# Fused attention, Fourier mixing and feed-forward on one core: a new written order, a third engine for the normalization, split first loads and an early exponential

## The chip, the cores and the metric

The kernel runs on one NeuronCore of a Trainium2 chip. The metric is the device time of one execution in microseconds (us). A NeuronCore has a matmul engine (TensorE, PE in the profile; PEld is its weight load), three engines for elementwise work (VectorE or DVE, ScalarE or ACT, GpSimd or POOL), and SyncE (SP), which here issues all DMAs. The engines run independently, each through its own list of instructions in sequence, and wait for each other on semaphores. Matmuls write to PSUM, eight banks, which GpSimd cannot read.

## The reference

```python
scores = scale * np.matmul(q, k.transpose(0, 1, 3, 2))
mask = np.triu(np.ones((seq, seq), dtype=bool), k=1)
scores = np.where(mask, -1000000000.0, scores)
scores = scores - np.max(scores, axis=-1, keepdims=True)
attn = np.exp(scores)
attn = attn / (np.sum(attn, axis=-1, keepdims=True) + 1e-09)
return np.matmul(attn, v).astype(np.float32)
...
X = np.fft.fft(x, axis=1)
X = np.fft.fft(X, axis=2)
mixed = np.real(X).astype(np.float32)
u = x + mixed
mu = np.mean(u, axis=-1, keepdims=True)
var = np.mean((u - mu) ** 2, axis=-1, keepdims=True)
un = (u - mu) / np.sqrt(var + 1e-06)
ch = np.maximum(un @ w_ch1, 0.0) @ w_ch2
return (u + ch).astype(np.float32)
```

Everything is float32: batch 4, 12 heads, sequence 448, head size 64. x is the attention's output with the heads side by side, 4 x 448 x 768; w_ch1 is 768 x 3072, w_ch2 is 3072 x 768.

## The kernel before

**Stages.** Two heads make a pair; there are 24 pairs (6 for each of 4 batches). For a pair, `attend` (L532) loads queries and keys as one tile raw and the values as v, scales the queries by -1/8 into qs (L553), and adds mask and scores in PSUM (units of rows 0 and 1 together, row 2, and the tail of both heads; L570). VectorE reduces each piece to mn (L594), ScalarE takes the exponential with the sum beside it (L607), VectorE makes the reciprocal ri (L615 to L621), p is normalized on one of three engines (L635), transposed in four groups on TensorE (L651), copied to pa (L657), multiplied by v (L661) and copied to xt (L674). When a batch's six pairs are there, `fold` (L678) adds and subtracts mirrored columns of xt, and `dft` (L706) does the two Fourier transforms as matmuls, adds the result to the transposed x (u, L775), and normalizes the four row groups of a batch: statistics (L781, L786), variance to the power -1/2 on GpSimd (L791, L792), u to un on VectorE or GpSimd (L801; before, all 16 are on VectorE), transposes of un (L811) and a store to DRAM.

The feed-forward part works with seven products in place of eight on 2 x 2 blocks, each block split into a high and a low part (`split`, L869), three matmuls for a product. `weights` (L824) loads half a chunk of a weight matrix (768 KB) and turns it from float64 to float32 with three activations on ScalarE (L833, L837, L850) and two operations on VectorE; 48 halves in all. `f1` (L994) multiplies un with w_ch1 chunk by chunk, each step in three thirds of three matmuls, keeps and adds partial sums c and applies the relu; `window` (L1132) multiplies by w_ch2 and adds into acc; `residual` and `store` end it. Attention takes the time up to about 220 us, `f1` goes on to about 550, `window` to the end.

**The order.** Each step is added to a plan as a unit (`Plan.add`, L389) with the engines that may do it, a cost and a due time. The costs and due times of the code are not used at run time: the tables RUN (L89), BY (L320), BANK (L362) and BUF (L369) hold the order of all 4,324 units, the engine of each, the PSUM banks and the buffers, written out. `order` (L398) checks that RUN keeps the data dependencies; units are then issued in RUN's order, so each engine's own list, SP's list of DMAs among them, is RUN cut down to that engine. A unit that waits holds up all later ones of its engine.

**The first units.** A memset and eleven warm-up matmuls (`warm`, L491); `consts` (L505) loads an identity, a mask and ones as one tile cst of 448 columns and casts it to bf16; GpSimd writes the constants eps; pair 0's keys (448 columns) and queries (512) are two loads, those of later pairs one of 960 columns (480 KB). The first two weight loads carry a mark that they come after the values of pair 10 (W_FROM, L44 and L830).

Of the kernel before, what the change touches and what calls it, by code (L numbers as in the profile page):

```python
# [1395 lines left out]
```

## Time and profile before

| | us |
|---|---|
| median of 3 runs (lowest, highest) | 862.75 (862.38, 864.58) |
| the profiled execution | 862.93 |
| its span, first to last instruction | 861.2 |

The profiled execution is 1.73 us longer than its span, for what lies around it, and 0.18 us above the median. A page sums up one profiled execution: busy time by engine, the span in slices, the chain of work that ended last. Further views give busy time by stretch, the instructions in order of time, who waited for whom, and the instructions of a line or tile grouped. In the rows, out<-in are the program's tile names, x is a count, and L is a line of the kernel.

### The profile page before, as it was taken

What the parts mean: (1) busy time and instruction counts of PE and PEld (TensorE: products, weight loads), DVE (VectorE), ACT (ScalarE), POOL (GpSimd) and SP (SyncE); (2) the same over time, 40 slices, a digit from 0 to 9 for tenths busy, and PEclk for the clock granted to TensorE, in tenths of its full rate; (3) what the DMA queues carried; (4) which work ended last, traced back from release to release, by engine and by line L of the source; (5) the groups of instructions that cost most, each with busy time, mean ns of one, the idle gap of its engine ahead of it and who ended that gap; (6) DMA issues with size and microseconds to landing.
All of it is one profiled execution on the core that took longest, in us unless ns stands there. A gap on an engine that the chain in (4) does not pass through costs nothing. (4 is left out here: it accounts for less than half of the span.)

```text
span 861.2 us, 15758 instructions
## 1 busy us (share of the span) xinstructions
PE 846.0 (98%) x5407; PEld 754.7 (88%) x5407; DVE 726.9 (84%) x1335; ACT 542.9 (63%) x1120; POOL 452.9 (53%) x466
## 2 busy tenths in 40 slices
...
GB/s 225 171 118 180 299 135 214 210 171 182 168 294 215 210 276 264 259 274 282 261 247 275 223 205 280 186 245 140 137 228 131 119 275 157 129 122 236 115 133 91
DMA packets 121359, 174.02 MB, mean 202 GB/s; under 512 B 21696, under 2 KB 98240, under 8 KB 121280
## 3 DMA queue, kind: packets, MB, share of 16 engines
...
## 5 line engine op out<-in xcount | busy, mean ns | idle before, releaser
L1184 PE MATMUL psum<-wa,w 128*128 128x384 f32 x1050 | 208.6, 336 | 0.5 <-DVE acc L1200 0.3
L1184 PEld LDWEIGHTS psum<-wa,w 128*128 128x128 f32 x1050 | 184.0, 188 | 1.7 <-issue 0.6
L1184 PE MATMUL psum<-wb,w 128*128 128x384 f32 x714 | 149.6, 336 | 0.0
L1184 PEld LDWEIGHTS psum<-wb,w 128*128 128x128 f32 x714 | 125.9, 188 | 0.2 <-DVE ue L1200 0.2
L1014 PE MATMUL psum<-0t,w 128*128 128x448 f32 x432 | 107.9, 366 | 2.1 <-DVE c L489 0.8
L1014 PE MATMUL psum<-1t,w 128*128 128x448 f32 x432 | 102.4, 363 | 0.9 <-ACT c L487 0.5
L850 ACT ACTIVATE w<-w 128x768 int8<-128x768 f32 x48 | 94.4, 1967 | 0.5
L876 POOL TENSOR_TENSOR w<-ws,w 128x384 fp32r<-128x384 f32 x57 | 64.5, 1139 | 53.4 <-DVE w L489 24.2
L608 ACT ACTIVATE p<-psum,mn 128x256 f32<-128x256 f32 (+3 forms) x168 | 83.2, 510 | 10.4 <-DVE mn L600 10.0
L1014 PEld LDWEIGHTS psum<-0t,w 128*128 128x128 f32 x432 | 79.9, 188 | 10.9 <-ACT c L487 3.3
L1014 PEld LDWEIGHTS psum<-1t,w 128*128 128x128 f32 x432 | 80.4, 187 | 8.2 <-ACT c L487 1.3
L487 ACT CAST w<-us 128x384 fp32r<-128x384 f32 x65 | 32.5, 516 | 77.5 <-PE psum L1184 49.0
L1200 DVE TENSOR_TENSOR acc<-psum,acc 128x384 f32<-128x384 f32 x96 | 51.1, 550 | 26.1 <-PE psum L1184 25.2
L487 ACT CAST w<-ws 128x384 fp32r<-128x384 f32 x81 | 39.9, 515 | 52.1 <-DVE ws L882 22.2
L876 POOL TENSOR_TENSOR w<-us,w 128x384 fp32r<-128x384 f32 x45 | 52.5, 1174 | 36.3 <-ACT w L487 22.4
L600 DVE TENSOR_REDUCE mn<-psum 128x1 f32<-128x448 f32 (+3 forms) x96 | 62.0, 665 | 10.6 <-PE psum L588 8.1
L588 PE MATMUL psum<-raw,qs 64*128 64x384 f32 (+3 forms) x336 | 66.5, 430 | 0.1
L642 POOL TENSOR_TENSOR p<-p,ri 128x128 f32<-128x128 f32 (+3 forms) x61 | 37.5, 635 | 39.7 <-DVE ri L620 35.2
L1040 DVE TENSOR_TENSOR c<-psum,c 128x448 f32<-128x448 f32 x69 | 42.7, 620 | 15.8 <-PE psum L1014 8.9
L1014 PE MATMUL psum<-ue,w 128*128 128x448 f32 x216 | 54.1, 365 | 0.0
L654 PEld LDWEIGHTS psum<-cst,p 128*128 128x128 f32 x384 | 42.6, 141 | 12.6 <-issue 3.8
L860 DVE SCALAR_TENSOR_TENSOR w<-w,w 128x768 uint32<-128x768 uint32 x48 | 49.6, 1033 | 4.5 <-ACT w L850 3.9
...
## 6 DMA issues: line engine op xcount, KB each, us to landing
...
```

What stands on the lines that cost most here:

```text
L487: nc.scalar.copy(out=out, in_=in_)
L588: nc.tensor.matmul(out=T[ps][:, at[r]:at[r] + n], lhsT=T[qs][s, q0:q0 + 128], rhs=T[raw][s, QW:QW + n], start=False, stop=y == len(rows) - ...
L600: nc.vector.tensor_reduce(out=z, in_=x, axis=AX, op=ALU.min)
L608: nc.scalar.activation(out=T[pb][:, PO[rr]:PO[rr] + n], in_=T[ps][:, c0:c0 + n], func=ACTF.Exp, scale=-1.0, bias=T[mn][:, rr:rr + 1], accu ...
L654: nc.tensor.transpose(T[ps][:, 128 * k:128 * k + 128], T[pb][:, e:e + 128], T["cst", 0][:, 0:128])
L850: nc.scalar.activation(out=T[w].bitcast(I8)[:, :, 3], in_=T[w][:, :, 1].bitcast(F32), func=ACTF.Prelu, scale=SIGN_SCALE, alpha=SIGN_ALPHA)
L860: nc.vector.scalar_tensor_tensor(out=T[w32], in0=T[w32], scalar=3, in1=T[w][:, :, int(join)], op0=ALU.logical_shift_left, op1=ALU.bitwise_or)
L876: (nc.gpsimd if eng == "G" else nc.vector).tensor_tensor(out=lo(), in0=src(), in1=hi(), op=ALU.subtract)
L1014: nc.tensor.matmul(out=T[ps][:, 0:S], lhsT=w[:, a, t], rhs=T[us[t]][:, b], start=first and k == 0, stop=last and k == 8, skip_group_check= ...
L1040: nc.vector.tensor_tensor(out=T[z], in0=T[ps][:, 0:S], in1=T[z], op=ALU.add)
L1184: nc.tensor.matmul(out=T[ps][:, 0:384], lhsT=T[hb][:, a, y], rhs=T[z][:, b], start=first and y + v == 0, stop=last and y == n - 1 and v == ...
L1200: nc.vector.tensor_tensor(out=x, in0=T[ps][:, 0:384], in1=x, op=ALU.add)
```

## The change

- **Order.** RUN, BY, BANK and BUF are written anew, for 4,330 units. Six units are new: one load and one cast for the split constants, two loads and one scaling for pair 0, and the early exponential. Of the old units 703 have another engine. TensorE's units keep their broad sequence; `f1`'s first third stands close to where it stood.
- **Normalization.** GpSimd makes two more products, mean times rstd and that times -1. With them un can be one activation on ScalarE (Identity with scale and bias). In the new BY it is ScalarE for 9 of 16 tiles (one of batch 0, two each of batches 1 and 2, all four of batch 3) and VectorE for 7. The copies of the first Fourier results (L730, L743) are on ScalarE 21 times instead of 13, those of pa 57 instead of 61, of xt 28 instead of 30, of ub 25 instead of 27, the normalizations of p 63 instead of 65.
- **First loads.** cst comes in two pieces (320 and 128 columns), pair 0's queries and keys in two each (256 and 256, 256 and 192). In the new RUN their order on SP is queries, constants, keys, then the second pieces of queries, keys and constants, then pairs 1, 2 and 3.
- **Early exponential.** GpSimd's constants move to the front, with a third (-1), and ScalarE takes the exponential of one of them as its first instruction.
- **Weights.** W_FROM is 0, so that the first weight loads only follow the values of pair 0. In the new RUN they stand behind pair 5's load and ahead of pair 6's.
- **Around the last pair.** Between the product of pair 23 (unit 1251, now 1257) and the first transposes of batch 3's x (unit 1274, now 1280) there was one TensorE unit; now there are ten, of `f1` and of transposes of un.

The tables are cut to their first lines here.

```diff
@@ -41,7 +41,7 @@
-C_FROM, W_FROM, N_WARM = 0, 10, 11
+C_FROM, W_FROM, N_WARM = 0, 0, 11
 N_W1, N_C, N_WS = 8, 3, 3
...
@@ -87,298 +87,298 @@
     ("y1", "t4", "a", 1, 0, False, True))
 
 RUN = (
-    0, 6, 2, 5, 43, 89, 1, 7, 126, 8, 3, 9, 16, 10, 13, 20, 45, 14, 17, 11, 46, 172, 44, 12, 15, 91, 49, 18, 21, 19,
-    47, 56, 22, 53, 48, 23, 92, 24, 50, 27, 25, 28, 29, 30, 31, 55, 36, 26, 52, 128, 32, 54, 37, 34, 33, 93, 38, 35,
...
+    0, 9, 2, 6, 8, 10, 7, 11, 1, 4, 49, 95, 132, 96, 133, 12, 13, 3, 15, 14, 22, 5, 19, 26, 21, 23, 20, 51, 25, 16,
+    52, 24, 27, 18, 55, 17, 53, 28, 97, 54, 29, 62, 56, 30, 57, 36, 35, 34, 98, 387, 59, 178, 33, 31, 37, 58, 42,
+    32, 61, 134, 38, 60, 43, 40, 39, 63, 44, 252, 41, 50, 101, 45, 99, 65, 108, 105, 64, 100, 102, 46, 215, 66, 67,
...
@@ -503,18 +503,25 @@
         add("PE", 600 + 427 * N_WARM, -4000, f, rd=[(*z, "warm")], wr=[ps], phase="A")
 
     def consts():
-        def f():
-            nc.sync.dma_start(out=T["cst", 0], in_=cc)
-        add("D", dma(128 * 4 * CW), -2498.5, f, wr=[("cst", 0)], phase="A")
-
-        def f(eng):
-            copy(eng, T["bfc", 0], T["cst", 0])
-        add(("S", "V", "G"), (acts(CW), dve(CW, 1.92), gps(CW)), -1898, f, rd=[("cst", 0)], wr=[("bfc", 0)], phase="A")
+        for key, c0, c1, p in (("b", 128, CW, -2498.5), ("a", 0, 128, -2300)):
+            def f(c0=c0, c1=c1):
+                nc.sync.dma_start(out=T["cst", 0][:, c0:c1], in_=cc[:, c0:c1])
+            add("D", dma(512 * (c1 - c0)), p, f, wr=[("cst", 0, key)], phase="A")
+
+            def f(eng, c0=c0, c1=c1):
+                copy(eng, T["bfc", 0][:, c0:c1], T["cst", 0][:, c0:c1])
+            n = c1 - c0
+            add(("S", "V", "G"), (acts(n), dve(n, 1.92), gps(n)), p + 600, f, rd=[("cst", 0, key)], wr=[("bfc", 0, key)], phase="A")
 
         def f():
             nc.gpsimd.memset(T["eps", 0][:, 0:1], 1e-6)
             nc.gpsimd.memset(T["eps", 0][:, 1:2], -0.5)
-        add("G", 80, 1000, f, wr=[("eps", 0)], phase="A")
+            nc.gpsimd.memset(T["eps", 0][:, 2:3], -1.0)
+        add("G", 80, -2600, f, wr=[("eps", 0)], phase="A")
+
+        def f():
+            nc.scalar.activation(out=T["eps", 0][:, 3:4], in_=T["eps", 0][:, 0:1], func=ACTF.Exp)
+        add("S", 1500, -2599, f, rd=[("eps", 0)], wr=[("eps", 0, "e")], phase="A")
 
     def tables():
         for k, nm in enumerate(("cd0", "cd1", "cs")):
@@ -540,23 +547,28 @@
             add("D", dma(512 * (c1 - c0)), p, f, wr=keys, phase="A")
 
         if i == 0:
-            load(QW, QW + S, [(*raw, "k")], base - 2500)
-            load(0, QW, [(*raw, "q")], base - 2499)
+            load(QW, QW + 256, [(*raw, "k")], base - 2500)
+            load(0, 256, [(*raw, "q")], base - 2499)
+            load(256, QW, [(*raw, "q1")], base - 2498)
+            load(QW + 256, QW + S, [(*raw, "k1")], base - 2497)
         else:
-            load(0, QW + S, [(*raw, "q"), (*raw, "k")], base - 2500)
+            load(0, QW + S, [(*raw, z) for z in ("q", "k", "q1", "k1")], base - 2500)
 
         def f():
             nc.sync.dma_start(out=T[v], in_=vv[b, t])
         add("D", dma(229376), base - 2495, f, wr=[v, ("go", i)], phase="A")
         sp = base + SPLIT_AT
 
-        def f(eng):
-            if eng == "S":
-                nc.scalar.mul(T[qs], T[raw][:, 0:QW], -0.125)
-            else:
-                (nc.gpsimd if eng == "G" else nc.vector).tensor_scalar(
-                    out=T[qs], in0=T[raw][:, 0:QW], scalar1=-0.125, scalar2=None, op0=ALU.mult)
-        add(("S", "V", "G"), (acts(QW), dve(QW, 1.92), gps(QW) + 216), sp, f, rd=[(*raw, "q")], wr=[qs], phase="A")
+        for k, (c0, c1) in enumerate(((0, 256), (256, QW)) if i == 0 else ((0, QW),)):
+            def f(eng, c0=c0, c1=c1):
+                x, z = T[raw][:, c0:c1], T[qs][:, c0:c1]
+                if eng == "S":
+                    nc.scalar.mul(z, x, -0.125)
+                else:
+                    (nc.gpsimd if eng == "G" else nc.vector).tensor_scalar(out=z, in0=x, scalar1=-0.125, scalar2=None, op0=ALU.mult)
+            n = c1 - c0
+            add(("S", "V", "G"), (acts(n), dve(n, 1.92), gps(n) + 216), sp + k, f, rd=[(*raw, "q1" if k else "q"), *([] if i == 0 else [(*raw, "q1")])],
+                wr=[(*qs, k)], phase="A")
 
         mn, sm, pb = ("mn", i), ("sum", i), ("p", i)
         rows_ = ROWS0 if i == 0 else ROWS
@@ -588,7 +600,8 @@
                         nc.tensor.matmul(
                             out=T[ps][:, at[r]:at[r] + n], lhsT=T[qs][s, q0:q0 + 128], rhs=T[raw][s, QW:QW + n],
                             start=False, stop=y == len(rows) - 1, skip_group_check=True)
-            add("PE", SC_COST[0 if tail else len(rows)], p0, f, rd=[qs, (*raw, "k"), ("bfc", 0)], wr=banks, phase="A", mode="F" if tail else "H")
+            add("PE", SC_COST[0 if tail else len(rows)], p0, f, rd=[*([(*qs, 0), (*raw, "k")] if i or k == 0 else [(*qs, 0), (*qs, 1), (*raw, "k"), (*raw, "k1")]), *([(*raw, "k1")] if i else []),
+                ("bfc", 0, "b"), *([("bfc", 0, "a")] if tail else [])], wr=banks, phase="A", mode="F" if tail else "H")
 
             for y, r in enumerate(rows):
                 def f(banks=banks, c0=at[r], n=KE[r], r=r):
@@ -652,7 +665,7 @@
                 for k, (r, c) in enumerate(blocks):
                     e = PO[r] + min(128 * c, KE[r] - 128)
                     nc.tensor.transpose(T[ps][:, 128 * k:128 * k + 128], T[pb][:, e:e + 128], T["cst", 0][:, 0:128])
-            add("PE", TR_COST, p0, f, rd=[*[(*pb, r, "n") for r in {r for r, _ in blocks}], ("cst", 0)], wr=[ps], phase="A")
+            add("PE", TR_COST, p0, f, rd=[*[(*pb, r, "n") for r in {r for r, _ in blocks}], ("cst", 0, "a")], wr=[ps], phase="A")
 
             def f(eng, ps=ps, g=g):
                 copy(eng, T[pa][:, 512 * g:512 * g + 512], T[ps])
@@ -788,9 +801,12 @@
                 add("V", 118, nxt(), f, rd=[(*st6, 0), (*st6, 1)], wr=[mv], phase="Q", port=False)
 
                 def f(w=w, st6=st6):
-                    nc.gpsimd.tensor_tensor(out=T[st6][0:w, 14:15], in0=T[st6][0:w, 13:14], in1=T["eps", 0][0:w, 0:1], op=ALU.add)
-                    nc.gpsimd.tensor_tensor(out=T[st6][0:w, 14:15], in0=T[st6][0:w, 14:15], in1=T["eps", 0][0:w, 1:2], op=ALU.pow)
-                add("G", 785, pr[0], f, rd=[mv, ("eps", 0)], wr=[rs], phase="Q")
+                    r = T[st6][0:w, 14:15]
+                    nc.gpsimd.tensor_tensor(out=r, in0=T[st6][0:w, 13:14], in1=T["eps", 0][0:w, 0:1], op=ALU.add)
+                    nc.gpsimd.tensor_tensor(out=r, in0=r, in1=T["eps", 0][0:w, 1:2], op=ALU.pow)
+                    nc.gpsimd.tensor_tensor(out=T[st6][0:w, 15:16], in0=T[st6][0:w, 12:13], in1=r, op=ALU.mult)
+                    nc.gpsimd.tensor_tensor(out=T[st6][0:w, 15:16], in0=T[st6][0:w, 15:16], in1=T["eps", 0][0:w, 2:3], op=ALU.mult)
+                add("G", 1300, pr[0], f, rd=[mv, ("eps", 0)], wr=[rs], phase="Q")
 
                 def f(w=w, ui=ui, u=u):
                     row = b * S + ui * R
@@ -798,10 +814,14 @@
                 add("D", dma(344064), pr[0] + 200, f, rd=ua, wr=[("ud", b)], phase="Q")
 
                 def f(eng, w=w, u=u, un=un, st6=st6):
+                    if eng == "S":
+                        nc.scalar.activation(
+                            out=T[un][0:w], in_=T[u][0:w], func=ACTF.Identity, scale=T[st6][0:w, 14:15], bias=T[st6][0:w, 15:16])
+                        return
                     (nc.gpsimd if eng == "G" else nc.vector).tensor_scalar(
                         out=T[un][0:w], in0=T[u][0:w], scalar1=T[st6][0:w, 12:13], scalar2=T[st6][0:w, 14:15],
                         op0=ALU.subtract, op1=ALU.mult)
-                add(("V", "G"), (590, 3150), pr[0], f, rd=[*ua, mv, rs], wr=[un], phase="Q")
+                add(("V", "G", "S"), (590, 3150, acts(768) + 93), pr[0], f, rd=[*ua, mv, rs], wr=[un], phase="Q")
                 for hf in range(2):
                     ps, ub = ("at", (b, ui, hf)), ("ub", (b, ui, hf))
```

## Rows read from the trace of the kernel before

**Rows 1.** The page: span, and busy us (share of the span) with instructions.

```profile
span 861.2 us, 15758 instructions
...
PE 846.0 (98%) x5407; PEld 754.7 (88%) x5407; DVE 726.9 (84%) x1335; ACT 542.9 (63%) x1120; POOL 452.9 (53%) x466
```

**Rows 2.** Busy us by stretch and engine, then granted clock, DMA share, GB/s.

```profile
0.00:20.00 20.00, 17.23 (x134) 9.13 (x136) 11.43 (x28) 11.28 (x37) 0.82 (x6) 1.00 0.71 242
20.00:60.00 40.00, 39.16 (x425) 27.40 (x422) 35.71 (x74) 34.38 (x117) 24.21 (x35) 1.00 0.37 112
60.00:200.00 140.00, 138.00 (x1265) 103.45 (x1264) 126.95 (x270) 123.48 (x335) 86.60 (x115) 1.00 0.63 208
200.00:260.00 60.00, 57.85 (x417) 46.72 (x416) 57.07 (x117) 52.59 (x123) 34.94 (x45) 1.00 0.73 219
260.00:560.00 300.00, 296.65 (x1471) 272.70 (x1470) 246.76 (x433) 214.44 (x310) 109.77 (x99) 1.00 0.75 247
560.00:861.20 301.20, 297.07 (x1708) 295.32 (x1706) 248.97 (x420) 106.71 (x203) 196.61 (x168) 1.00 0.51 161
```

The columns are PE, PEld, DVE, ACT and POOL, each with its count of instructions.

**Rows 3.** First 15 us in order of time: start, us, engine, instruction, [idle before].

```profile
1.64 1.37 SPq L539 DMA_DIRECT2D raw<-in_qk_dram  x3
...
5.98 0.50 PE L581 MATMUL psum<-bfc 64*128 64x128 bf16 x8
6.59 0.52 PEld L588 LDWEIGHTS psum<-raw,qs 64*128 64x128 f32 x8 [0.32 <-DMA raw<-in_qk_dram]
...
7.35 0.25 PE L581 MATMUL psum<-bfc 64*128 64x128 bf16 x4
...
7.59 1.02 DVE L600 TENSOR_REDUCE mn<-psum 128x2 f32<-128x256 f32 x2 [3.20 <-PE psum L588]
8.26 0.20 PE L581 MATMUL psum<-bfc 128*128 128x64 bf16 x1
...
8.70 1.28 ACT L608 ACT_TABLE_LOAD   x1 [8.70 <-DVE mn L600]
...
9.99 0.47 ACT L608 ACTIVATE p<-psum,mn 128x256 f32<-128x256 f32 x1
...
14.55 0.33 PE L654 MATMUL psum<-cst,p 128*128 128x128 f32 x1
```

**Rows 4.** Prices: grouped instructions by line; first two with min/median/max ns, first and last start.

```profile
L833 ACT ACTIVATE w<-w x48: 874/908/1069, 70.1 to 704.0; 128x768 f32<-128x768 f32 x48
L850 ACT ACTIVATE w<-w x48: 1925/1965/2079, 70.9 to 671.8; 128x768 int8<-128x768 f32 x48
...
L801 DVE TENSOR_SCALAR un<-u,st 112x768 f32<-112x768 f32 (+1 forms) x16 | 11.5, 716 | 0.7 <-POOL st L792 0.7
...
L791 POOL TENSOR_TENSOR st<-st,eps 112x1 f32<-112x1 f32 (+1 forms) x16 | 4.9, 305 | 14.4 <-DVE st L786 13.4 <-DVE ri L616 0.7
...
L487 ACT COPY pa<-psum 128x512 f32<-128x512 f32 x61 | 34.5, 604 | 4.8 <-PE psum L654 4.6
L638 ACT ACTIVATE p<-p,ri 128x128 f32<-128x128 f32 (+3 forms) x65 | 32.6, 549 | 5.2 <-DVE ri L620 5.2
...
L487 ACT COPY xt<-psum 128x224 f32<-128x224 f32 x30 | 9.5, 361 | 0.5 <-PE psum L664 0.5
...
L555 ACT ACTIVATE qs<-raw 128x512 f32<-128x512 f32 x9 | 5.9, 656 | 0.0
...
L487 ACT COPY yb<-psum 112x386 f32<-112x386 f32 (+1 forms) x4 | 1.9, 476 | 0.0
```

The other seven have busy us, mean ns of one, and the idle time before them with what ended it.

**Rows 5.** TensorE's waits, 200 to 260 us: us in total, times, longest.

```profile
PE psum L765 <- ACT xt L487: 1.1, 1, 1.1
PE psum L722 <- DVE f L701: 0.4, 1, 0.4
PE psum L1014 <- DVE u L775: 0.4, 1, 0.4
```

**Rows 6.** Busy us by engine from 20 to 65 us, columns as in rows 2.

```profile
20.00:65.00 45.00, 44.16 (x454) 31.95 (x451) 39.63 (x83) 37.29 (x127) 27.73 (x39) 1.00 0.44 142
```

More of the change, by code (lines that the diff above doesn't have):

```diff
@@ L362 @@
-BANK = (
-    "15612025315345671725602367763760340154734501232543301267457040236271250104174206454660671204722056011063653401"
-    "74553467232570260145434547012355101340054322060321603225665756017507526723203436016751577167673561551201503253"
-    "67123533625223323565001673725776360167705352016771650301673733506712256567012367151501232707072710351156127270"
-    "57437574332106715024736423015723413016726514207314056204317405126305124063125676341037424510576227040562771457"
-    "30623143057376456275036342102475716201376204754523072")
@@ new lines @@
+BY = (
+    "VPDVDGGSDDDDDVVPVSSVSSPVSSPVSVVGGSGSVVPSPSPVPSPVSDDVPVSPVSSVSSPVSSVVSGGGGVVPSPSPVPVPVVGGGGVGGGGDDVPVSPVSSVSSPV"
+    "SSVVGGGVVSSPSPVPSPSPVSDDGPVSPVSSVSSPVSSVVVGGSGGSPVPSPVPSPVVGGGVGGGVGDDVPVSPVSSVSSPVSSVVSVVGVGGPSPSPSPVPVSDDSPV"
+    "SPVSSVSSPVSSVVVVSGSSSPSPSPVPSPVVDDDGGGGVVVVVPPSPPSPSPVVPVVPVVVGDVPSDPSDPVVPVVVGDVPSDPSDPPSPPSPSPVVPVVPVVVGDSPS"
+    "DPVDPVVPVVVGDVPVDPVDDDSPVSPVSSVSSPVSSVVGGVSSGVPVPVPVPVPVSDDSPVSPVSSVSSPVSSVVGSVVVSVPVPSPSPSPSSGGGGGGGGGDDVPVSP"
+    "VSSVSSPVSSVVGGSSSGSPSPVPSPVPSVDDSPVSPVSSVSSPVSSVVSVGVGVVPVPSPVPSPSSGGGGGGGVVDDVPVSPVSSVSSPVSSVVGGGGGVGPVPVPVPS"
+    "PSSDDVPVSPVSSVSSPVSSVVSGGGSVSPVPVPSPSPSSGGGVVVGGGPPSPPVPSPVVPVVPVVVGDVPSDPSDPVVPVVVGDSPSDPVDPPSPPSPVPVVPVVPVVV"
+    "GDSPSDPVDPVVPVVVGDVPSDPSDDDGPVSPVSSVSSPVSSVVVGGVVSGPVPVPSPSPSVDDVPVSPVSSVSSPVSSVVSGGVVVSPSPVPVPVPVVGGGGGGVGGDD"
+    "VPVSPVSSVSSPVSSVVGGGVSSSPVPVPSPSPSVDDSPVSPVSSVSSPVSSVVGSGSGSSPSPVPSPSPVVGGGVGVGVVDDSPVSPVSSVSSPVSSVVVGSGVSSPSP"
+    "VPSPSPSSDDGPVSPVSSVSSPVSSVVVSGVSGSPVPSPSPSPVVGGGVVGVGGPPSPPSPSPVVPVVPVVVGDSPSDPSDPVVPVVVGDSPSDPSDPPVPPSPSPVVPV"
+    "VPVVVGDVPSDPSDPVVPVVVGDVPSDPSDDDGPVSPVSSVSSPVSSVVVGVSGSVPSPSPSPVPSSDDVPVSPVSSVSSPVSSVVSSSSGVGPSPSPSPSPSSGGGVGG"
+    "GGGDDSPVSPVSSVSSPVSSVVGSSSSGSPVPSPSPVPVSDDSPVSPVSSVSSPVSSVVVSSSGVSPSPSPVPSPSSGGGVVVVGVDDVPVSPVSSVSSPVSSVVSGGGS"
+    "VSPSPVPVPSPSSDDSPVSPVSSVSSPVSSVVSSSVSVSPVPSPSPSPSSGGGVVVVVVPPSPPSPSPVVPVVPVVVGDSPSDPSDPVVPVVVGDSPVDPVDPPSPPSPS"
+    "PVVPVVPVVVGDSPSDPSDPVVPVVVGDSPSDPSDDDDDVGVDVDVDSVGDDDDDSGVDGDVDVGGDDDDDVVGDGDVDVGGDDSSSVVDDSSSVVDSVVVVVSVSVVSV"
+    "VSVSVDSVDSVDSVDSVDSVDSVDSVDSVDSGDSVDSGDSVDSGDSGDSGDSSSVVDDSSSVVDSVSVVVSGSVVVVGSVSGPPPSPPPVSDPPPSPPPPPPSVSDPPPV"
+    "SDPPPVDDDDDSVVSVSVVSVVSVSGVSVDDDDSVVSVSVVSVVSVSVVSGDDDDSVVSVSVVSVVSVSVVSVDSSSVVDDSSSVVDSGSVVVSVVVVSGVSVSVPPPSP"
+    "PPVVDPPPSPPPPPPSVSDPPPVSDPPPSDDSSSVVDSSSVVSVSVVVSVSVGSVVSGSGPPPSPPPVSDPPPSPPPPPPSVSDPPPVSDPPPSDPPPSPPPSPPPVVDP"
+    "PPVSDPPPSPPPSPPPPPPPPPSVSDPPPSVSDPPPVVDPPPVSDPPPVDPPPVDDSSSVVDSSSVVSVDDSVDDVVVVSGDDSVDDSVDDVVDDSVDDDSSSVVDSSSV"
+    "VVVSVVVVVSGVVVVVVVGPPPVPPPSPPPVSDPPPVVDPPPVPPPSPPPPPPPPPSVSDPPPSVVDPPPVSDPPPVSDPPPVDPPPVDDSSSVVDSSSVVVGVVVGVGV"
+    "VVSGVSGVGDSSSVVDSSSVVVGDDSVDDVGGVVGDDSGDDSVDDSVDDVGDDPPPSPPPSPPPVVDPPPVVDPPPSPPPSPPPPPPPPPVVSDPPPSVSDPPPVVDPPP"
+    "VSDPPPVDPPPSDDSSSVVDSSSVVVVSVVVSVSGGVGVSGVVDSSSVVDSSSVVSVDDVVDDGGVGVGDDVGDDSGDDVGDDSGDDPPPVPPPSPPPVVDPPPVVDPPP"
+    "SPPPVPPPPPPPPPSVSDPPPSVVDPPPVVDPPPVSDPPPSDPPPVDDSSSVVDSSSVVSGSGVGVGVGVSVGVGVVPPPSPPPVPPPVVDPPPVSDPPPSPPPSPPPPP"
+    "PPPPSVVDPPPVVVDPPPVVDPPPVSDPPPVDPPPSDDSSSVVDSSSVVVGDDVGDDGGGGSGDDSGDDVGDDSVDDSGDDDSSSVVDSSSVVSGVGGGSVVVVVVVSGV"
+    "VPPPSPPPSPPPVSDPPPVSDPPPVPPPVPPPPPPPPPVVSDPPPVVSDPPPVVDPPPVSDPPPVDPPPVDDSSSVVDSSSVVSVVGGVVGVGVVGGSVVGDSSSVVDSS"
+    "SVVSGDDSVDDGGVGVVDDSGDDSVDDVVDDSGDDPPPSPPPVPPPVSDPPPVVDPPPVPPPSPPPPPPPPPSVVDPPPVVVDPPPVSDPPPVSDPPPSDPPPSDDSSSV"
+    "VDSSSVVVVSVVVVVVVGVVVSVVGDSSSVVDSSSVVVVDDVVDDGVGVVGDDVVDDSGDDSGDDSVDDPPPVPPPSPPPVVDPPPVSDPPPSPPPVPPPPPPPPPSVSD"
+    "PPPVVSDPPPVSDPPPVVDPPPSDPPPVDDSSSVVDSSSVVVVSVVGSGSGGVVGSVSVPPPSPPPVPPPVVDPPPVVDPPPVPPPSPPPPPPPPPVVSDPPPSVVDPPP"
+    "VSDPPPVVDPPPSDPPPSDDDSGVVVGSVSGVVGVSGSVDDSGVVVVSVSGVSVVVVSGPPPSPPPVSDPPPSPPPPPPSVSDPPPVSDPPPSDDDDDDDDDSSSVVDSS"
+    "SVVVVSGVGGVSGSVSGSGSGDSSSVVDSSSVVSVVGGGVGSVSVVVSVVGDDVVSGVVSVSVVSGVSGVGPPPSPPPVSDPPPSPPPPPPVVVDPPPVSDPPPVDPPPS"
+    "PPPVSDPPPSPPPPPPSVVDPPPVSDPPPSDDDDDSVSGVVVVVVVVVGSVSVPSPVPSPSPVPVPSDDDDVGSVGVSVSVVSVGSVVGPSPVPSPSPVPVPVDDDDSVS"
+    "VGGSGSGVSGVSGSGPSPVPVPSPVPVPVDDDDSVSGVVSGSVGSVGVGSVPVPVPSPSPVPVPSDDDDSVSVGGSGSVVVVVSVSVPSPVPSPSPVPVPSDDDDDDDDS"
+    "SSVVDSSSVVSVSVVVVVSVSGSGVGSVDSSSVVDSSSVVSGSVVVVVVVSVVGSVSVDDDDSVSVVGSVSVVSVGVGSVPSPVPVPSPVPVPSDDDDSVSGVVSGSGGS"
+    "VVSVSVPSPVPVPSPVPVPSDDDDSGSGGGSVVGVSVGSGSGPVPVPVPVPVPVPVDDDDSVSGVGSGSGVSGGSGSGPVPVPVPVPVPVPVDVDDDDSGSVGVSVVGGV"
+    "GVSGSVPVPVPVPVPVPVPVDVDDDDSVSGGVSVSVGSVVSGVGPVPVPVPVPVPVPVDGDDDDSVVGGVSGSVGSVVSVSGPVPVPVPVPVPVPVDDDDDDDDSSSVVD"
+    "SSSVVSVSVGGVGSGSGSGSVSVDDDDDDDDVDDDDSVSVVGSGSVGSGGSGSVPVPVPVPVPVPVPVDVDDDDSGSGVVSGSGGVVGSVVGPVPVPVPVPVPVPVDVDD"
+    "DDSVSGVGSGSVVSGVSVSVPVPVPVPVPVPVPVDVDDDDSVSGGGSGSVGSGGSVSGPVPVPVPVPVPVPVDVDDDDSGSGVVVVSVVSVVSGSGPVPVPVPVPVPVPV"
+    "DGDDDDSGSVVGSGSGVVGGSVVGPVPVPVPVPVPVPVDGDDDDSVSVVVSGSGVVVVSGSVPVPVPVPVPVPVPVDDDDDDDDSSSVVDSSSVVVGSVVVVVSVVGSVS"
+    "VSGDDDDDDDDGDDDDSGSVGVVVSGVSGGSGSVPVPVPVPVPVPVPVDGDDDDSVSGGVVGSVVSVVSGSGPVPVPVPVPVPVPVDVDDDDSGSVGVSGSGVSVGSVVV"
+    "PVPVPVPVPVPVPVDGDDDDDDDDVVSGGGVVSGVVVGSGSGPVPVPVPVPVPVPVDDDDDDDDVVSVVGSGSGVSGGSGVVPVPVPVPVPVPVPVDDDDDDDDSVSVVG"
+    "SGSGVSGGSGSGPVPVPVPVPVPVPVDDDDDDDDSVVGGVSGSGGSGGSVSVPVPVPVPVPVPVPVDDDDDDDDSVSVVVSVSGGVVGSVSVPVPVPVPVPVPVPVDDDD"
+    "DDDDSGSGGGSVSGGVGVSGSGPVPVPVPVPVPVPVDDDD")
@@ new lines @@
+BANK = (
+    "41256725141045671276202345634710346707067056345407331245710224024015070105207434325043671207343456451427661223"
+    "75322567342701360156434557012334300030612675130257557503621756012751326712341576124534605034677766731201362553"
+    "56013276203730606216225332766775220167612333015661125512670201256756556767012305767501230511002351271637007670"
+    "30550604112636415024736421015723413016726514207314056244317405126305104721056037051573540722567104552406510314"
+    "35607374055451602574310725165307641055163256743654024")
```

65 lines of the change are left out of this document (13 added, 52 removed), and 453 rows, old and new, of the table RUN.

## The prediction

> **What bounds the kernel now.** I read the page first, then busy time by stage, the first 15 us in order of time, the waits of one stage, and the prices of single instructions. The page says that TensorE works in 98% of an 861.2 us span [rows 1]; the stage table gives its granted clock as 1.00 in every stretch, the level of 2.4 GHz [rows 2]. So only TensorE's idle time can be won, and what lies hidden in stretched instructions. The stage table says where it idles: TensorE's busy time taken from each stretch leaves 2.8 us in 0 to 20, 0.8 in 20 to 60, 2.0 in 60 to 200, 2.15 in 200 to 260, 3.35 in 260 to 560 and 4.1 after that [rows 2]. Together these are 15.2 of 861.2 us, and no edit removes a matmul. In the same table VectorE works 57.07 of the 60 us from 200 to 260 and ScalarE 52.59: there the helpers set the pace. After 560 ScalarE works 106.71 of 301.20, so what it is given there costs nothing.
>
> The start is a chain [rows 3]. Behind the warm-up matmuls the first scores are issued at 5.98, and their second half waits 0.32 us for the keys; two reductions run from 7.59; ScalarE loads its table from 8.70, since its first instruction waited for them; its first exponential starts at 9.99, and the first transpose of pair 0, which needs all seven and their normalization, at 14.55.
>
> **The change part by part**, against the profiled execution (862.93 us, 0.18 above the median of 862.75).
>
> *Start.* The early exponential moves the table load off the path, from 8.70 to 9.98, into idle time before it: gain 1.28 [rows 3]. It waits for memsets at the head of GpSimd's list and is over before 4 us, so it costs 0. The Trainium skill ("ScalarE: Activation LUTs", What ACT_TABLE_LOAD costs) counts 2.66 us for a switch, with a drain of some 1.38 beside the load. By that the start would gain 1.4 us more; the row has the exponential 0.01 us behind the load, and I go by the row.
> The scores of rows 0 and 1 need only 256 columns of keys and of queries. With the pieces the bytes up to these keys fall from 704 KB to 416 KB by the code's widths, so the wait of 0.32 goes: gain 0.3. The new order lets one reduction over 512 columns go first and its exponential right behind it, where two (1.02 us together) stood in front: gain 0.4. Sum of the start: 1.28 + 0.3 + 0.4 = 2.0 us. From the first exponential to the first transpose the path is of the same length, and TensorE's seven score units until then stand in the same sequence, so the 2.0 reach it. Bounds: 0, if the next reductions come too late to feed ScalarE; and 2.2, since a unit that nothing hinders (7.35 to 8.26 [rows 3]) takes 0.91, and seven of these fill 6.4 of the 8.6 us from 5.98 to 14.55.
> The pieces put three more DMA issues on SP ahead of pair 1's load. Three issues took 1.37 us [rows 3], so this load leaves 1.4 later, behind the same bytes; its scaling on VectorE stands behind a reduction until about 8.8 (an estimate) anyway. Cost 0, at worst 0.6.
>
> *Normalization on ScalarE.* Nine of the 16 tiles leave VectorE, where one takes 716 ns; on ScalarE I price them by the 128x768 activation, 908 ns by the median, 8.2 us in all [rows 4]. Five of the nine lie in 200 to 260. The two products that GpSimd gains take 305 ns each by the addition beside them [rows 4], 0.6 us more on the chain of a tile. GpSimd is idle for 25 of those 60 us [rows 2], and other units stand between a tile and its transposes. Cost 0, at worst 0.6 once.
>
> *The order from 200 to 260.* Three waits make up 1.9 of the 2.15 us: 1.1 for ScalarE's copies of the last pair, 0.4 each for VectorE's folded rows and its u [rows 5]. Before, one TensorE unit of 0.6 us stood between the last pair's product and the transposes that need these copies; the new order has ten there, some 5 us, so the 1.1 goes. The two waits for VectorE I let go too, for the five tiles, 3.6 us, that it loses there. Gain 1.9; bounds 0 (ScalarE's copies late behind its four tiles of batch 3, which is what comes late next) and 2.15.
>
> *Weights from the outset.* The first two weight loads (768 KB each) leave some 35 us earlier (an estimate from the places in the list). They pass pair 6's load on SP, which is wanted some 14 us later (an estimate from TensorE's units between), and the DMA engines are 63% free from 20 to 60 [rows 2]. Cost 0, at worst 0.5. Of their six conversions on ScalarE which began at 70.1, five now stand before 65: four of about 0.91 and one of 1.97 us, 5.6 us [rows 4].
> Up to 65 us other moves count as well: ScalarE gains four scalings of q (656 ns), two copies of pa (604) and two of Fourier results (476), and loses five copies of xt (361) and three normalizations of p (549) [rows 4]: 4.8 - 3.5 = 1.3. Together it gets 6.9 us more, and it idles 45.00 - 37.29 = 7.7 there [rows 6]. It fits, but in scraps. I take a cost of 0.4; bounds 0 and 6.9 (nothing fits). From 65 to 260 the moves cancel: nine tiles and six more Fourier copies come, the conversions, six copies of pa and four scalings go.
>
> *The rest of the order.* Of 4,324 units 703 change engine, and TensorE's units trade places, most by a few. From 260 to 560, 3.35 us idle behind copies of c and conversions; the same kinds of unit stand there as before. I take 0; bounds -2 and +2, a little over half of it either way.
>
> Sum: 2.0 + 1.9 - 0.4 = 3.5 us. 862.75 - 3.5 = **859.2 us**. What a measurement of this kernel can tell from no change is 0.3%, 2.6 us: faster means below 860.2, slower above 865.3.
>
> **The rivals.**
> *Only the start.* The waits from 200 to 260 move instead of going: 862.75 - 2.0 = 860.8. For it: both helpers are nearly full there. Against: ten units in place of one.
> *Waits fall everywhere.* The new order also halves the 2.0 us of 60 to 200 and the 3.35 of 260 to 560: 859.2 - 2.7 = 856.5. For it: only order and queues stand behind these waits. Against: ScalarE and VectorE have the same work to do in sum.
> *It does not do what it says.* The table loads early, but TensorE meets the same queues later and waits the 2.0 us there: 862.7. Against: ScalarE's own work starts 2 us earlier too.
> *Slower: ScalarE becomes the bound from 20 to 65.* It works in sequence, so exponentials and evictions queue behind a conversion of 1.97 us. If nothing of the 6.9 us fits its idle time, TensorE waits 6.9 and the start gives back 2.0: 862.75 + 4.9 = 867.7. It decides once more than 4.6 of the 6.9 fit nowhere. Against: the 7.7 us idle, and that no matmul needs these weights before 130.
>
> **How the numbers follow.** Forecast 0.46, only the start 0.23, waits fall everywhere 0.17, nothing 0.07, slower 0.07. Faster: 0.42 of the forecast, the 0.17, and 0.03 of "only the start": 0.62. Slower 0.07, same 0.31. The range goes from 855.3, a little beyond "waits fall everywhere", to 862.2, which is "only the start" with 1.4 us of the costs above (0.6, 0.4 and 0.4); outside remain "nothing", "slower" and the tails.
>
> **What would show it.** Right: a table load before 4 us, a first exponential near 8.0 and a first transpose of pair 0 near 12.5; no wait for xt near 220; under 0.5 us idle in the stretch that was 200 to 260. Wrong: a second table load, which would mean that the normalization needs another set; TensorE waiting for ScalarE by over 3 us in sum from 20 to 65; waits for c and for conversions from 260 to 560 that outweigh the old 3.35.

## The result, and the profile after

The changed kernel takes 849.31 us (median of 4; 848.93 to 850.34) where the kernel before takes 862.71 beside it: a ratio of 0.9842 (95% interval 0.9825 to 0.9859). It is 13.4 us faster; 3.5 were predicted, and 849.3 lies outside the range. The page after, first line and busy times, against [rows 1]:

```profile
span 847.7 us, 15801 instructions
...
PE 840.2 (99%) x5407; PEld 755.7 (89%) x5407; DVE 711.7 (84%) x1300; ACT 556.2 (66%) x1148; POOL 472.9 (56%) x509
```

The span fell by 13.5 us. TensorE's idle time fell from 15.2 to 7.5, by 7.7; the other 5.8 us are in its busy time, 846.0 before and 840.2 now for the same 5,407 matmuls. Some matmuls of before were long because they stood waiting, and the busy time counted that. Busy time by stretch of the changed kernel, columns as in [rows 2]:

```profile
0.00:20.00 20.00, 17.70 (x140) 9.59 (x141) 12.52 (x28) 13.85 (x46) 5.75 (x16) 1.00 0.79 264
20.00:60.00 40.00, 40.00 (x432) 30.00 (x431) 33.79 (x76) 37.96 (x113) 25.61 (x35) 1.00 0.44 157
60.00:200.00 140.00, 139.84 (x1311) 105.46 (x1311) 126.24 (x273) 128.59 (x358) 90.73 (x142) 1.00 0.62 199
200.00:260.00 60.00, 59.45 (x406) 51.11 (x403) 57.32 (x118) 54.88 (x117) 27.70 (x43) 1.00 0.77 233
260.00:560.00 300.00, 299.08 (x1501) 277.71 (x1500) 251.06 (x431) 216.35 (x320) 129.02 (x113) 1.00 0.76 250
```

TensorE's idle time is 0 from 20 to 60 us, 0.16 to 200, 0.55 to 260, 0.92 to 560. The first 14 us of the changed kernel in order of time, against [rows 3]:

```profile
0.72 1.28 ACT L523 ACT_TABLE_LOAD   x1 [0.72 <-PEq L1373]
...
5.55 0.34 PE L593 MATMUL psum<-bfc 64*128 64x128 bf16 x8
...
7.41 0.47 ACT L621 ACTIVATE p<-psum,mn 128x256 f32<-128x256 f32 x1 [5.20 <-DVE mn L613]
...
9.43 1.02 PE L600 MATMUL psum<-raw,qs 128*128 128x448 f32 x2 [0.98 <-DVE qs L568]
...
13.39 0.87 PE L667 MATMUL psum<-cst,p 128*128 128x128 f32 x6
```

The table load is off the path, the first exponential comes 2.58 us earlier, the first transpose 1.16. From 260 to 560 us, what the waits of TensorE (PE) hide, those of its weight load (PEld) show: it stops when an operand is late, while the matmul ahead of it goes on being counted. The kernel before, five rows of PEld and PE's own for the first of them:

```profile
PEld psum L1014 <- ACT c L487: 4.2, 8, 0.9
PEld psum L1014 <- DVE w L876: 1.5, 3, 0.8
PEld psum L1014 <- DVE c L1040: 1.5, 4, 0.5
PEld psum L1014 <- DVE c L489: 1.3, 2, 1.2
PEld psum L1014 <- DVE us L489: 0.6, 1, 0.6
...
PE psum L1014 <- ACT c L487: 1.2, 3, 0.5
```

and the changed kernel (its first five):

```profile
PEld psum L1034 <- DVE c L1060: 1.8, 4, 0.8
PEld psum L1034 <- ACT c L487: 0.7, 2, 0.4
PEld psum L1034 <- ACT c L1068: 0.7, 1, 0.7
PEld psum L1034 <- DVE w L896: 0.6, 2, 0.4
PEld psum L1034 <- DVE 1112_3768 L896: 0.5, 1, 0.5
```

9.1 us of such waits became 4.9 with three more of 0.2, where PE's own idle time of before was 3.35 [rows 2]. This is no measure for other stretches: from 60 to 200 us PEld's waits for other engines sum to some 11 us in both kernels, though the table below has 10.0 us lost there before and 6.3 now.

To see where the time was won I made one table from the records of each kernel. For each of TensorE's units I take the time from its first matmul to that of the next unit, less what a unit of its kind takes when nothing hinders it (0.60 us for a third of an `f1` step, 0.92 for the scores of rows 0 and 1, and so on); the sum is the time lost so far. Progress is the sum of the unhindered times, so that a line compares the same amount of work. us lost:

```
progress  before  after  a_old  h1    h2    h3    h4    h5    k
  20        4.5    2.7    3.1   2.1   2.8   4.0   3.1   2.2   4.4
  60        7.2    4.1    6.5   3.5   4.2   7.4   6.5   3.6   5.8
 200       17.2   10.4   16.2  13.6  10.4  17.0  13.3   9.8  12.1
 260       24.0   13.4   24.3  21.8  13.4  25.0  16.2  13.1  14.7
 300       24.9   15.6   25.1  22.6  18.8  25.6  18.4  15.2  16.9
 520       29.8   16.5   29.8  26.7  23.0  26.4  19.2  17.0  17.8
 820       31.2   17.9   31.5  27.9  24.2  27.5  20.4  18.7  18.9
```

The lead of the changed kernel is 1.8 us at 20, 3.1 at 60, 6.8 at 200, 10.6 at 260 and 13.3 at the end. By kind, `f1` lost 11.4 and now 6.6, the transposes of p 6.2 and 2.9, the scores of rows 0 and 1 3.2 and 1.1. Before, 36 units with 0.2 us or more lost each held 17.8 us; now 17 hold 6.9. So it is a matter of a few dozen single stalls.

### The profile page after: what moved, and what is told of

The parts are those of the page before. It is cut to its first block, busy times and chain, and to the rows that moved or that the text cites. A ratio compares the mean times of both kernels' runs of the same rounds, so it can differ in the third digit from the quotient of the medians.

```text
span 847.7 us, 15801 instructions
## 1 busy us (share of the span) xinstructions
PE 840.2 (99%) x5407; PEld 755.7 (89%) x5407; DVE 711.7 (84%) x1300; ACT 556.2 (66%) x1148; POOL 472.9 (56%) x509
## 4 chain that ended last, share of the span: by engine, by line
PE 90%; DVE 4%; DMA 2%; ACT 2%; issue 1%; POOL 0%; SPq 0%; DVEq 0%; ACTq 0%
PE psum L1204 35%; PE psum L1034 31%; PE psum L600 6%; PE psum L677 5%; PE psum L667 5%; PE psum L735 3%; PE psum L593 1%; PE psum L752 1%; PE psum L778 1%; PE psum L831 1%; DMA raw<-in_qk_dram 1%; DMA us<-und 1%; DVE w L896 1%; DMA w<-in_w_dram 0%; DVE us L902 0%
## 5 line engine op out<-in xcount | busy, mean ns | idle before, releaser
L896 POOL TENSOR_TENSOR w<-ws,w 128x384 fp32r<-128x384 f32 x58 | 67.1, 1162 | 59.6 <-ACT w L487 46.2
L487 ACT CAST w<-us 128x384 fp32r<-128x384 f32 x77 | 38.5, 513 | 80.9 <-PE psum L1204 34.6
L487 ACT CAST w<-ws 128x384 fp32r<-128x384 f32 x86 | 44.3, 519 | 47.5 <-PE psum L1204 25.9
L896 POOL TENSOR_TENSOR w<-us,w 128x384 fp32r<-128x384 f32 x40 | 46.9, 1175 | 31.1 <-ACT w L487 16.9
L880 DVE SCALAR_TENSOR_TENSOR w<-w,w 128x768 uint32<-128x768 uint32 x48 | 53.0, 1105 | 3.0 <-ACT w L870 2.4
L1060 DVE TENSOR_TENSOR c<-psum,c 128x448 f32<-128x448 f32 x69 | 42.3, 617 | 13.5 <-PE psum L1034 7.9
```

Source lines behind the costliest of these rows:

```text
L487: nc.scalar.copy(out=out, in_=in_)
L880: nc.vector.scalar_tensor_tensor(out=T[w32], in0=T[w32], scalar=3, in1=T[w][:, :, int(join)], op0=ALU.logical_shift_left, op1=ALU.bitwise_or)
L896: (nc.gpsimd if eng == "G" else nc.vector).tensor_tensor(out=lo(), in0=src(), in1=hi(), op=ALU.subtract)
```

## The experiments

OLD and NEW stand for the tables of the two kernels; the old order is written in the new units. Each time is a median, beside 862.7 to 863.2 for the kernel before on the same chip. In the table a_old is a_old_order, k is k_late_table, and h1 to h5 are the runs whose names begin so.

**The code without the plan.**

```diff
-RUN, BY, BANK, BUF = NEW
+RUN, BY, BANK, BUF = OLD
```

> All four code changes, but the order, the engines, the banks and the buffers of before (the new units stand at the front, un stays on VectorE). Theory 'sequence' (the gain lies in where each unit stands in its engine's list): only the start is gained, 1.5 to 2.5 us, so 860 to 861. Theory 'engines' (VectorE works 15 us less, 726.9 to 711.7): the same, 860 to 861, since the engines are the old ones. Theory 'code' (pieces, exponential and GpSimd's products are what does it): 850 to 853.

Measured: 862.95 us, ratio 0.9998 (0.9988 to 1.0007). The start's gain is there, 1.4 us at 20 in the table, still 1.0 at 200, and gone at 260 (column a_old). It is lost from 200 to 260, where VectorE is full [rows 2], and among TensorE's waits there is a new one of 1.0 us for a tile of GpSimd's. That tile, 0t, comes right behind the two products that the code adds for the normalization:

```profile
PE psum L1025 <- POOL 0t L887: 1.0, 1, 1.0
```

```profile
246.09 0.19 POOL L798 TENSOR_TENSOR st<-st 113x1 f32<-113x1 f32 x1
246.36 0.55 POOL L799 TENSOR_TENSOR st<-st,eps 113x1 f32<-113x1 f32 x1
246.86 1.13 POOL L887 TENSOR_TENSOR 0t<-us,0t 128x448 fp32r<-128x448 f32 x1
```

So by the trace what is left of the lead goes for these products, which the old order has no use for; the old order without them was not run. The code alone is worth nothing; the time is won by the plan.

**Order or engines alone.**

```diff
-RUN, BY, BANK, BUF = NEW
+RUN, BANK, BUF = NEW; BY = OLD
```

> The new sequence, banks and buffers, but every old unit on the engine it had before; so un is on VectorE for all 16 tiles. Sequence: most of the 13.4 us stays, 850 to 854. Engines: the gain goes except for the start, 859 to 862. If the two only work together (703 units stand where their new engine is free, not their old one), slower than either kernel: over 863.

```diff
-RUN, BY, BANK, BUF = NEW
+RUN, BANK, BUF = OLD; BY = NEW
```

> The mirror image: the sequence, banks and buffers of before, with the new engines (9 tiles of un on ScalarE) and all code changes. Engines: 850 to 854. Sequence: 859 to 862. If the two only work together: over 863.

Measured: 905.85 and 926.99 us, ratios 1.0498 (1.0481 to 1.0516) and 1.0729 (1.0706 to 1.0752). TensorE's longest sums of waits with the old engines, then with the old order:

```profile
PE psum L1034 <- DVE c L489: 6.2, 5, 2.4
PE psum L667 <- ACT p L621: 4.1, 6, 1.5
```

```profile
PE psum L1025 <- DVE c L1051: 7.4, 10, 2.5
PE psum L1195 <- DVE acc L1211: 7.2, 9, 2.3
```

These are the ordinary evictions. Ahead of the longest of the first row (2.4 us) VectorE had stood 2.71 us for a weight from ScalarE, with the copy of c two places further down its list:

```profile
336.60 0.56 DVE L896 TENSOR_TENSOR w<-w,w 128x384 fp32r<-128x384 f32 x1 [2.71 <-ACT w L487]
```

That the others, too, stand behind work that the order did not put there is argued and not shown. An order is written for one choice of engines and holds for that alone: the new order with the old engines costs 43 us, the old order with the new ones 64, and together the new ones win 13.

**Normalization back on VectorE** (nine units of BY).

```diff
-BY = NEW
+BY = NEW, with "V" for "S" in the units of un
```

> The kernel after, with the nine tiles of un back on VectorE at the same places in the order (9 times 716 ns more there). If VectorE is what sets the pace from 60 to 260, 3 to 6 us slower than after: 852 to 855. If the choice matters little, under 1 us: 849 to 850.5.

Measured: 852.50 us, ratio 0.9873 (0.9859 to 0.9888), some 3 us over the changed kernel; the two intervals just touch. In the trace it is 0.8 us behind the changed kernel at 220 in progress, 2.8 at 260 and 2.3 at the end. TensorE's waits from 200 to 260, where the changed kernel has the last two alone:

```profile
PE psum L831 <- DVE u L788: 1.0, 1, 1.0
PE psum L831 <- DVE c L1060: 0.6, 1, 0.6
PE psum L752 <- ACT ya L487: 0.4, 1, 0.4
PE psum L677 <- ACT pa L487: 0.2, 1, 0.2
```

The c of the second row stands directly behind a moved tile in VectorE's list:

```profile
248.53 1.24 DVE L821 TENSOR_SCALAR un<-u,st 112x768 f32<-112x768 f32 x1
249.69 0.61 DVE L1060 TENSOR_TENSOR c<-psum,c 128x448 f32<-128x448 f32 x1
```

The u of the first row has a moved tile further up in a list without a gap, at 240.65. So this order needs the third engine.

**The start, part by part.**

```diff
-            nc.scalar.activation(out=T["eps", 0][:, 3:4], in_=T["eps", 0][:, 0:1], func=ACTF.Exp)
+            pass
```

> The changed kernel with the exponential of a constant left out (its output is used by nothing), all else as it is. Theory 1, the start's chain (scores, largest value, exponential, transposes) sets the lead that lasts to the end, as the sum had it: the table load of 1.28 us goes back in front of the first real exponential, 849.3 + 1.0 to 1.3 = 850.3 to 850.6 us, with the same waits later. Theory 2, TensorE has other work there and only the visible start moves: within 0.4 us of 849.3.

Measured: 850.86 us, ratio 0.9861 (0.9848 to 0.9875), which overlaps the changed kernel's interval. But it did not take away what it was made to take away. ScalarE's first instructions there:

```profile
0.72 1.28 ACT L621 ACT_TABLE_LOAD   x1 [0.72 <-PEq L1373]
8.04 0.47 ACT L621 ACTIVATE p<-psum,mn 128x256 f32<-128x256 f32 x1 [6.04 <-DVE mn L613]
```

The load still stands at 0.72. In the kernel before, the first exponential waits for VectorE and for TensorE; the first wait is taken by the load ahead of it. In the new order it waits for VectorE alone, by itself, and the load runs free. So the run says nothing on the load. It is 1.5 us above the changed kernel all the same, and what makes that is open. The next run puts the load back; in RUN its unit also moves 17 places down, to right ahead of the first real exponential:

```diff
-            nc.scalar.activation(out=T["eps", 0][:, 3:4], in_=T["eps", 0][:, 0:1], func=ACTF.Exp)
+            nc.scalar.activation(out=T["eps", 0][:, 3:4], in_=T["mn", 0][:, 1:2], func=ACTF.Exp, bias=T["eps", 0][:, 0:1])
```

> The changed kernel, but the exponential of a constant reads the first largest values instead of a constant and is issued right before the first real exponential, so that the table load waits for VectorE as it did in the kernel before. The first exponential then starts at 7.41 + 1.28 + 0.2 = 8.9 us. If the start's chain sets the lead (the prediction's 1.28 us): 850.6 to 851.0 us, against 849.3. If TensorE is covered there by the scores of the next pair: 849.1 to 849.8 us.

Measured: 850.65 us, ratio 0.9858 (0.9843 to 0.9873): 1.3 over the changed kernel, the number of the first theory.

```profile
7.19 1.28 ACT L514 ACT_TABLE_LOAD   x1 [7.19 <-DVE mn L604]
8.49 0.30 ACT L514 ACTIVATE eps<-mn,eps 128x1 f32<-128x1 f32 x1
8.69 0.46 ACT L612 ACTIVATE p<-psum,mn 128x256 f32<-128x256 f32 x1
```

The activation starts 0.02 us behind the end of the load. The Trainium skill ("ScalarE: Activation LUTs", What ACT_TABLE_LOAD costs) adds a drain of some 1.38 us; no run here shows one. The interval overlaps that of the changed kernel, and b_no_early_exp, with the load out of the way, lies as far above it, so the times do not show what the load costs. The trace loses 1.7 more by 20 and 1.0 more by the end, but the 1.28 us are not handed on as the sum had it. TensorE waits 0.5 us more, for an exponential, and then the scores of pair 1 take longer at a lower granted clock (last section). The wait, and the same four matmuls here and in the changed kernel:

```profile
PE psum L584 <- ACT p L612: 0.5, 1, 0.5
```

```profile
12.29 1.70 PE L591 MATMUL psum<-raw,qs 64*128 64x384 f32 x4
```

```profile
11.38 0.89 PE L600 MATMUL psum<-raw,qs 64*128 64x384 f32 x4
```

Pair 0's loads and the constants whole again:

```diff
-            load(QW, QW + 256, [(*raw, "k")], base - 2500)
-            load(0, 256, [(*raw, "q")], base - 2499)
...
+            load(QW, QW + S, [(*raw, "k")], base - 2500)
+            load(0, QW, [(*raw, "q")], base - 2499)
```

> The changed kernel with the first loads whole again (keys, queries and constants of pair 0 in one piece each), the order otherwise as it is. Theory 1, the pieces save what the prediction took for them (the keys' wait 0.3 and one reduction 0.4): 850.0 us. Theory 2, what the pieces save is lost to pair 1's load, which they send 1.4 us later and for which TensorE then waits 1.0 us: 848.6 to 849.4 us.

Measured: 849.84 us, ratio 0.9851 (0.9838 to 0.9865). 0.5 us is less than these runs can tell. The first exponential came at 7.84 instead of 7.41, and the wait for pair 1's queries fell from 0.98 to 0.40. But seven other runs whose first 70 us are written as the changed kernel's (c, g1, g2, g5, h1, h2 and h5) have the first exponential between 7.02 and 7.96, this wait between 0.4 and 1.6 and the first transpose between 12.72 and 13.65. One profiled execution of each cannot tell the two starts apart, so what the pieces win is not shown.

Pair 1's load one place earlier:

```diff
-    0, 9, 2, 6, 8, 10, 7, 11, 1, 4, 49, 95, 132, 96,
+    0, 9, 2, 6, 8, 10, 7, 11, 1, 49, 4, 95, 132, 96,
```

> The changed kernel with the load of pair 1's queries and keys issued one place earlier, ahead of the second piece of the constants. If TensorE's wait of 1.0 us at 9.4 us (pair 1's scores, for that load) sets the lead: 848.4 to 848.9 us. If the constants then come late for the first transposes, or the wait only moves on to the first transposes at 13.4 us: 849.0 to 849.8 us.

Measured: 849.62 us, ratio 0.9849 (0.9836 to 0.9863), its five executions from 849.1 to 852.4. The profiled one, 852.4, has this wait in its start:

```profile
PE psum L584 <- POOL bfc L480: 3.3, 1, 3.3
```

The second piece of the constants landed at 9.89 us instead of 5.79 behind the 480 KB. So this is no better version. And little of what the new plan loses at 10 us comes back later: its span is 2.9 us longer than that of the changed kernel.

**Grafts: the one plan up to a seam, the other behind.** Up to a seam both orders have done the same units but for 3 or 4, so that they can be joined:

```diff
-RUN, BY = NEW
+RUN = NEW[:1815] + [n for n in OLD if n not in NEW[:1815]]
+BY = NEW up to the seam, OLD behind
```

and likewise at 410 units (72 us) and 3,039 (520 us), and the other way round. In the first five each tile behind the seam got its old place if that was free, or else any free one.

> The new order, engines and tile places for the first 410 units (to about 72 us), the old ones for all that is behind them. The changed kernel reaches this point 3.2 us earlier than the kernel before. Theory 1, each stretch of the new plan gains by itself and a lead, once made, is kept: 862.7 - 3.2 = 859.5 us. Theory 2, the old order behind gives a lead back, as it did in a_old_order between 220 and 260 us: 862.4 to 863.0. Rival, a seam between two plans costs a wait of its own of over 2 us: above 863.

> The reverse of g1_new_to_72: the old plan for the first 410 units (with the new code of the start), the new one behind. Theory 1: 849.3 + 3.2, less the 0.7 us that the new start kept at this point in a_old_order: 851.8 to 852.5 us. Theory 2 (the new plan behind absorbs a late start, or needs the early one): 849.5 or above 854.

> The new order, engines and tile places for the first 1,815 units (to about 287 us, behind the transform of batch 3), the old ones behind. The changed kernel reaches this point 8.8 us earlier. Theory 1 (gains add stretch by stretch): 862.7 - 8.8 = 853.9 us, and 4.5 us of the gain comes from 287 us on. Theory 2 (only the whole plan is fast): 860 to 863.

> The reverse of g2_new_to_287: the old order, engines and tile places for the same 1,815 units, the new ones behind. Theory 1: 849.3 + 8.8 = 858.1 us. Theory 2 (what is behind gains only on what lies ahead of it): 861.5 to 863.

> The new order, engines and tile places for the first 3,039 units (to about 520 us), the old ones behind. The changed kernel reaches this point 12.3 us earlier, and from here on the two plans lose the same: the lead is 12.3 us at 520 and 13.3 us at the end. Theory 1 (each stretch's gain is its own, and a lead is kept): 862.7 - 12.3 = 850.4 us, up to 852 with a seam like that of g1_new_to_72. Theory 2 (only the whole plan is fast, the losses of the other grafts were not their seams): 855 or above, as g2_new_to_287 gave.

Measured:

| | us | sum of stretches | ratio (95% interval) |
|---|---|---|---|
| g1 | 861.34 | 859.5 | 0.9983 (0.9973 to 0.9993) |
| g4 | 853.94 | 851.8 to 852.5 | 0.9904 (0.9885 to 0.9924) |
| g2 | 857.33 | 853.9 | 0.9941 (0.9927 to 0.9956) |
| g3 | 859.97 | 858.1 | 0.9968 (0.9957 to 0.9980) |
| g5 | 854.54 | 850.4 | 0.9902 (0.9885 to 0.9918) |

All lie 1.4 to 4.1 us above the sum, between the two theories. In g5 the surplus had one place. A load on SyncE's queue, then busy time from 615 to 630 us:

```profile
SPq L1155 <- DVE ws L893: 10.0, 1, 10.0
```

```profile
615.00:630.00 15.00, 12.13 (x63) 11.84 (x63) 11.19 (x23) 5.46 (x11) 3.58 (x4) 0.92 0.65 212
```

A load stood 10.0 us for its buffer with all loads behind it, and 6 us later TensorE idled 2.9 us. The old plan would not have put the tile there. So the last runs keep order and engines, and rename the later plan's buffers as a whole, so that each load waits for the same reader as in its own plan:

```diff
-BUF = a free place for each tile behind the seam
+BUF = OLD behind the seam, buffers renamed one to one
```

> Order and engines of g5_new_to_520, but the old plan's tile places behind the seam are kept as a pattern (its buffers renamed as a whole), so that each load waits for the same earlier reader as in the kernel before. Theory 1 (stretches add, the surplus of g5_new_to_520 was made by the free choice of places): 850.4 to 851.5 us, and no idle TensorE near 623 us. Theory 2 (only the whole plan is fast): 854 to 855 again.

> The same for g2_new_to_287. Theory 1: 853.9 us, up to 855 with a small seam. Theory 2: 857 to 858 again.

> The same for g3_old_to_296. Theory 1: 858.1 us, up to 859. Theory 2: 860 again.

> Order and engines of g4_old_to_75, with the new plan's tile places behind the seam renamed as a whole (those of the raw inputs and the PSUM banks as in g4_old_to_75). Theory 1 (stretches add): 851.8 to 852.5 us. Theory 2 (part of the gain is the whole plan's): 853.9 us again.

> The same for g1_new_to_72 (the places of the raw inputs and the PSUM banks are those of g1_new_to_72). If the old order behind gives part of a lead back (1.4 us between 220 and 260 us in g1_new_to_72, as in a_old_order) whatever the places: 860.5 to 861.5 us again. If that was the places too: 859.5 us.

Measured:

| | us | sum of stretches | ratio (95% interval) |
|---|---|---|---|
| h5 | 850.43 | 850.4 | 0.9861 (0.9846 to 0.9875) |
| h2 | 856.23 | 853.9 | 0.9932 (0.9915 to 0.9949) |
| h3 | 857.89 | 858.1 | 0.9949 (0.9934 to 0.9964) |
| h4 | 852.07 | 851.8 to 852.5 | 0.9875 (0.9859 to 0.9892) |
| h1 | 860.61 | 859.5 | 0.9976 (0.9966 to 0.9986) |

The same stretch of h5:

```profile
615.00:630.00 15.00, 15.00 (x88) 14.80 (x87) 14.54 (x29) 6.43 (x13) 6.21 (x6) 1.00 0.75 235
```

h5, h3 and h4 came out at the sum of their stretches (an interval reaches 0.9 to 1.5 us to either side). h1 lies 1.1 above it; between 220 and 260 it has a_old_order's wait for GpSimd's 0t again, 0.9 us. h2 lies 2.3 above its sum, 1.2 above the end of its range; its seam has one wait, behind one queue: three conversions of weights of 1.95, 0.97 and 1.91 us meet on ScalarE, one after another, ahead of a copy of c:

```profile
PE psum L1025 <- ACT c L478: 2.4, 1, 2.4
```

The table says the same by columns. From 60 to 820 the old order loses 24.0 us and h1, which follows it there, 24.4; the new one 13.8, h4 13.9. From 300 on: old 6.3, h2 5.4; new 2.3, h3 1.9. From 520 on: 1.4 each, h5 1.7. But for the seams and that wait, what a plan loses in a stretch is its own, whatever came before. The gains of h1 and h4 (2.3 and 10.7) make 13.0 of 13.4 us, though h4 also has 0.7 that the new code wins at the start; those of h2 and h3 (6.6 and 5.0) make 11.6.

Not tried, and so open, is which of the moved units in a stretch removed which stall; with order and engines each useless alone, there is no smaller part of this plan that I could take out.

## Why the prediction was right in its direction and wrong in its size

**The failed step** is "*The rest of the order* ... I take 0; bounds -2 and +2". The lead grows by 3.7 us from 60 to 200 and by 2.7 from 260 on: 6.4 of the 13.3. The reason given, that the same kinds of unit stand there as before, holds, and a_old_order, e and f show that kinds of unit decide nothing: the same units cost 863, 906 or 927 us by their order and engines. The bounds failed as well, since they were taken from TensorE's visible idle time, 3.35 us from 260 to 560, where the weight load's waits were 9.1. The text did say that time "lies hidden in stretched instructions", and then left it out of the sum.

**The start** (2.0): the lead at 20 is 1.8. Right in size, but not shown by its parts, so luck has a share. The early exponential is not what moves the load: the new order does so alone (b_no_early_exp). With the load back on the path the trace lost 1.7 by 20, by a wait of 0.5 us and slower scores and not as 1.28 us down the chain, and how much of it lasts the times do not show (k_late_table). "Cost 0, at worst 0.6" for pair 1's load was too small: it landed at 8.93, its scaling was ready 0.4 later, and TensorE waited 0.98 (0.4 to 1.6 in the seven runs named at d_whole_loads). The first transpose came at 13.39 instead of near 12.5: 1.16 reached it, where the sum handed on 2.0.

**Normalization on ScalarE** (cost 0): a tile takes 1042 ns, longer than its price of 908, GpSimd's two products less than 305 each. The Trainium skill ("ScalarE: Activation LUTs", What ACT_TABLE_LOAD costs) counts 93 ns for each operand read by a pointer, of which this activation has two, so 186. The rows show 1042 - 908 = 134 for both, over an activation that differs in its input as well, so they do not settle it.

```profile
L818 ACT ACTIVATE un<-u,st 112x768 f32<-112x768 f32 (+1 forms) x9 | 9.4, 1042 | 0.0
...
L808 POOL TENSOR_TENSOR st<-st,eps 112x1 f32<-112x1 f32 (+1 forms) x16 | 4.1, 257 | 1.2
...
L807 POOL TENSOR_TENSOR st<-st 112x1 f32<-112x1 f32 (+1 forms) x16 | 3.3, 209 | 1.3
```

In the new order the cost was rightly 0; in the old one the two products hold TensorE up by 1.0 us (a_old_order). What the change wins (some 3 us, c_un_vector) was counted only as "The two waits for VectorE I let go too", 0.8 us.

**The order from 200 to 260** (1.9): the wait for xt is gone, as forecast, and 0.55 us is idle in that stretch, just over the 0.5 named as a sign. The lead grows by 3.8: twice the term, since the visible waits were not all that was lost there.

**Weights from the outset** (cost 0.4): no cost. From 20 to 65 us, against [rows 6]:

```profile
20.00:65.00 45.00, 45.00 (x463) 34.38 (x462) 36.63 (x84) 41.87 (x124) 25.64 (x35) 1.00 0.39 140
```

ScalarE got 4.6 us more instead of 6.9, and TensorE idled not at all. The lead grew by 1.3 from 20 to 60. The slower rival fell here.

**The rivals.** "Waits fall everywhere" named what happened, with 0.17. Sized from the visible idle time it could not reach the result: with all of the 2.0 and 3.35 us gone it gives 859.2 - 5.35 = 853.9. None of the three signs of being wrong came: one table load, no idle TensorE from 20 to 65 us, less waiting from 260 to 560. They looked at the same visible waits and could not have warned of a gain this large. "It does not do what it says" is what the code alone does (a_old_order).
